# The stores of a finished token block: from SyncE's DMA queue to GpSimd's

## The chip, the cores and the metric

The kernel runs on one core of a Trainium2 chip. The metric is the time of one execution on the device, in microseconds, from the first to the last instruction of the core. Engines: PE is TensorE's matmul, PEld its weight load, DVE is VectorE, ACT is ScalarE, POOL is GpSimd, SP is SyncE. SyncE computes nothing here; it issues transfers.

## The reference, cut to what matters

```
x: (2048, 512); C_re, C_im: (2048, 2048); D_re, D_im: (512, 512); w1, w3: (512, 1376); w2: (1376, 512)
a = C_re @ (x @ D_re.T) - C_im @ (x @ D_im.T)          # real part of a two-dimensional Fourier transform
b = (silu(x @ w1) * (x @ w3)) @ w2                      # gated feed-forward half
g = sigmoid((x * gate_w).sum(-1))                       # one gate for each token
out = g * a + (1 - g) * b                               # (2048, 512), float32
```

The kernel swaps the order of the two transforms: it forms Z = C x first (the sequence transform, re and im), and then y = Z D.

## The kernel before, in words

A float32 product is made of three TensorE passes. Each operand v is split into hi (v rounded to fewer bits, a ScalarE copy, L77) and lo = v - hi (a VectorE subtraction, L83), and hi*hi + hi*lo + lo*hi is accumulated in PSUM (`mm3`, L87). So whatever TensorE reads has passed through ScalarE and VectorE first.

The program has three stages. The first is the feed-forward half, which ends at about 339 us of the span and leaves b in a DRAM buffer, `bsp`. The second is the sequence transform, from 339 to 652 us. The third is y = Z D with the gated sum.

The sequence transform works on four blocks of 512 tokens (tb). A block has 16 steps: g = 0 with p = 0 to 7 and g = 1 with p = 0 to 7. Each step multiplies one group of rows of the sequence matrix, in Winograd's form of Strassen's algorithm, so that a block makes seven products P1 to P7; g = 0 feeds P1, P3, P6, P5 (24 TensorE passes in a step) and g = 1 feeds P2, P7, P4 (18 passes). `fourier_step(n)` for step n does four kinds of work in the program's text:

- `load_c(n + 4)` loads 768 KB of the matrix: `cu` (512 KB, L445 or L448) and `cv` (256 KB, L446 or L449), both on SyncE's queue. They go into staging tiles of one pool of 13 buffers (`f4`), which other loads share.
- `sums_c(n + 2)` forms sums of the loaded parts on VectorE (L469, L470 for g = 0; L472, L473 for g = 1).
- `prep_c1(n + 2)` and `prep_c2(n + 2)` split the results into the tiles `zo` (four buffers) which TensorE reads.
- `zprod` issues TensorE's products.

At the last step of g = 0, ScalarE copies P1 into `s1` (shown as zs, L542), and VectorE forms `u2` (zu, L556), `u4` (zu, L558) and `c12` (c, L561); c12 is finished and stored by `spill` (L520). At the last step of g = 1, VectorE adds P7, P2 and P4 (L583, L584, L587, L590), and u4, s1 and u2 are stored in that order. Each of the four stores writes a tile of 128 x 1024 float32, 512 KB, to the DRAM buffer `zsp`. The tiles s1, u2, u4 and c12 have one buffer each (pool `ut`), so the next block may write such a tile only after its store has read it. The output tiles `o` of the last stage use the same four buffers.

`zsp` is read back by `load_z` (L609, tile zr) for the third stage: the first rows during the last steps of the fourth block, the others while y is computed. There `bsp` is loaded into `o` (L650), scaled by ScalarE (L651), and VectorE forms the output (L653), which goes out on ScalarE's queue and, for the last half tile, SyncE's.

The order of the instructions on each engine is set when the program is built: a scheduler places them by priority and by when buffers come free, and each engine then runs its list in that order. A DMA issue waits at the head of its engine's queue until its data and its buffer are ready, and everything behind it on that engine waits too. Each DMA also uses one of eight semaphores in turn, so it waits until the DMA eight places before it has landed. GpSimd issues no DMA before the change.

Of the kernel before, what the change touches and what calls it, by code (L numbers as in the profile page):

```python
# [12 lines left out]
P = 128  # L13
S = 2048
D = 512
# [13 lines left out]
def fnet_swiglu_gate_kernel(  # L29
# [9 lines left out]
    gw: bass.AP,  # L39
    out: bass.AP,  # L40
):
    """A float32 product is three passes: each operand v is split exactly into
    hi = v rounded to 12 significant bits and lo = v - hi, and hi*hi + hi*lo +
    lo*hi is accumulated in float32.

    The gate and up products are one 2x2x2 block product (gate | up weights by
    halves of D by two token blocks) in the seven products of Winograd's form of
    Strassen's algorithm, and so is the transform along the sequence (halves of
    D by halves of the sequence by re | im)."""
    nc = tc.nc  # L50

    def pool(name, bufs, side, space=None):
        kw = {} if space is None else {"space": space}
        cm = tc.tile_pool(name=name, bufs=bufs, side=side, reuse_waits="tile", **kw)
        return cm, cm.__enter__()
# [14 lines left out]
    def bank(k, name):  # L70
        return psum.tile([P, 512], F32, tag=f"ps{k}", name=name)

    def wide(name):
        return f4.tile([P, 1024], F32, tag="f4", name=name)

    def split(hi, lo, src, neg=False):
        nc.scalar.activation(hi, src, AF.Copy, scale=-1.0 if neg else 1.0)  # L77
        if neg:
            nc.vector.scalar_tensor_tensor(
                lo, src, -1.0, hi.bitcast(F32), op0=ALU.mult, op1=ALU.subtract  # L80
            )
        else:
            nc.vector.tensor_sub(lo, src, hi.bitcast(F32))  # L83

    def mm3(ps, ah, al, bh, bl, first, last, chain=False):
        for n, (u, v) in enumerate(((ah, bh), (ah, bl), (al, bh))):
            nc.tensor.matmul(ps, u, v, start=first and n == 0, stop=last and n == 2,  # L87
                             skip_group_check=chain)
# [5 lines left out]
    bsp = dram.tile([S, D], F32, tag="bsp", name="bsp")  # L94
    zsp = dram.tile([4 * NTB * P, 1024], F32, tag="zsp", name="zsp")

# [1 line left out]
    XO, ST = {}, {}  # L98

    def load_xo(g, t, j):  # L100
        """Half j of the staged operands t of token blocks 2g and 2g+1."""
        if g not in ST:
            ST[g] = [[wide(f"xs{g}_{q}_{i}") for i in range(4)] for q in range(2)]
            XO[g] = [xo.tile([P, 2, 7, 512], F32R, tag="xo", name=f"xo{g}_{q}") for q in range(2)]
        for q in range(2):
            nc.sync.dma_start(ST[g][q][t][:, j * 512 : (j + 1) * 512],
                              xt[g, q, :, t * 1024 + j * 512 : t * 1024 + (j + 1) * 512])

    # moving operands B11 B21 B22 T1 T2 T3 -T4 and where they are staged
    AT = {"B12": (0, 0), "B11": (0, 1), "B21": (1, 0), "B22": (1, 1),  # L110
          "T1": (2, 0), "T2": (2, 1), "T3": (3, 0), "T4": (3, 1)}
    OPS = ("B11", "B21", "B22", "T1", "T2", "T3", "T4")
# [25 lines left out]
                          w13[i % NC, :, lo * 256 : hi * 256])  # L138

    def prep_wa(i, lo=0, hi=3):  # L140
        """A11 A12 A22"""
        if lo == 0:
            WA[i] = wo.tile([P, 2, 3, 256], F32R, tag="wa", name=f"wa{i}", bufs=LOOK + 1)
        t = WA[i]
        split(t[:, 0, lo:hi].rearrange("p a n -> p (a n)"),
              t[:, 1, lo:hi].rearrange("p a n -> p (a n)"),
              WS[i][:, lo:hi].rearrange("p a n -> p (a n)"))

    def prep_wb(i, part=None):
        """S1 S2 S3 S4"""  # L150
        if part != 1:
            w = WS.pop(i)
            u = wo.tile([P, 4, 256], F32, tag="wu", name=f"wu{i}", bufs=1)
            nc.vector.tensor_add(u[:, 0], w[:, 3], w[:, 2])
            nc.vector.tensor_sub(u[:, 1], u[:, 0], w[:, 0])
            nc.vector.tensor_sub(u[:, 2], w[:, 0], w[:, 3])
            nc.vector.tensor_sub(u[:, 3], w[:, 1], u[:, 1])
            WB[i] = u
        if part != 0:
            u = WB[i]  # L160
            t = wo.tile([P, 2, 4, 256], F32R, tag="wb", name=f"wb{i}")
            split(t[:, 0].rearrange("p a n -> p (a n)"), t[:, 1].rearrange("p a n -> p (a n)"),
                  u.rearrange("p a n -> p (a n)"))
            WB[i] = t

    def prod(ps, i, wi, xi, start, chain=False):
        g = i // NC
        w, wi = (WA[i], wi) if wi < 3 else (WB[i], wi - 3)
        for q in range(2):
            sl = slice(q * P, (q + 1) * P)  # L170
            x = XO[g][q]
            mm3(ps, w[:, 0, wi, sl], w[:, 1, wi, sl], x[:, 0, xi, :], x[:, 1, xi, :],
                start and q == 0, q == 1, chain)
# [8 lines left out]
        G[i] = (x, s1)  # L182

    def first2(i):
        """the gate of the first block is P1 + P2"""
        y = bank(4 + i % 2, f"Y{i}")
        prod(y, i, 1, 1, True)
        s1 = G[i][1]
        nc.vector.tensor_add(s1, s1, y)
        nc.scalar.activation(s1, s1, AF.Silu)  # L190
# [88 lines left out]
    nc.scalar.activation(score[:, :1], warm[:, :1], AF.Silu)  # L279

    def plain(b12, a21):
        """The first chunk in eight products: they need no sums."""
        c = {}

        def half(i, j, w, x, start):
            if start:
                c[i, j] = bank((0, 4, 6, 7)[2 * i + j], f"C{i}{j}")
            for r in range(2):
                sl = slice(r * P, (r + 1) * P)
                mm3(c[i, j], w(0, sl), w(1, sl), x(r, 0), x(r, 1), start and r == 0,  # L290
                    not start and r == 1)

        def wa(k):
            return lambda h, sl: WA[0][:, h, k, sl]

        def xb(k):
            return lambda q, h: XO[0][q][:, h, k, :]

        w21 = lambda h, sl: a21[:, h, sl]
        x12 = lambda q, h: b12[:, h, q * 512 : (q + 1) * 512]  # L300
        s1 = tp.tile([P, 512], F32, tag="s1", name="s1_0", bufs=LOOK + 2)
        g1 = tp.tile([P, 512], F32, tag="g1", name="g1_0")
        h = wide("h0")
        H[0] = h
        yield half(0, 0, wa(0), xb(0), True)
        yield half(1, 0, w21, xb(0), True)
        half(0, 0, wa(1), xb(1), False)
        nc.scalar.activation(s1, c[0, 0], AF.Silu)
        yield half(1, 0, wa(2), xb(1), False)
        nc.vector.tensor_mul(h[:, :512], s1, c[1, 0])  # L310
        half(0, 1, wa(0), x12, True)
        yield half(1, 1, w21, x12, True)
        half(0, 1, wa(1), xb(2), False)
        nc.scalar.activation(g1, c[0, 1], AF.Silu)
        half(1, 1, wa(2), xb(2), False)
        yield nc.vector.tensor_mul(h[:, 512:], g1, c[1, 1])

    load_w(0, 0, 1)
    load_xo(0, 0, 1)
    load_w(0, 1, 4)  # L320
    load_xo(0, 1, 0)
    load_xo(0, 0, 0)
    load_w(1)
    load_xo(0, 1, 1)
# [4 lines left out]
    b12 = dn.tile([P, 2, 1024], F32R, tag="ho", name="b12")  # L329
    a21 = dn.tile([P, 2, 512], F32R, tag="w2o", name="a21")  # L330
    step = plain(b12, a21)
    prep_wa(0, 0, 1)
    split_xo(0, "B11")
# [72 lines left out]
    gate_up(NC, 2 * NC)  # L406
    close(xo_cm, wo_cm, tp_cm)

# [1 line left out]
    # rows d (halves) by [re | im] columns t, reduced over s (halves)  # L410
    a2_cm, a2 = pool("a2", 1, "left")
    zo_cm, zo = pool("zo", 4, "left")
    a1_cm, a1 = pool("a1", 1, "left")
# [3 lines left out]
    def flat(ap):  # L417
        return ap.rearrange("p a n -> p (a n)")

    def load_a(p):  # L420
        """A11 S1 S2 S4 | A12 A22 S3 of the rows s of tiles p and p + 8."""
        r = wide(f"xr{p}").rearrange("p (a n) -> p a n", a=4)
        m = wide(f"xm{p}").rearrange("p (a n) -> p a n", a=4)
        nc.sync.dma_start(flat(r), xn[p])
        a21, a11, a12, a22 = (r[:, i] for i in range(4))
        nc.vector.tensor_add(m[:, 0], a21, a22)
        nc.vector.tensor_sub(m[:, 1], m[:, 0], a11)
        nc.vector.tensor_sub(m[:, 2], a12, m[:, 1])
        nc.vector.tensor_sub(m[:, 3], a11, a21)
        split(A1[p][:, 0, 0], A1[p][:, 1, 0], a11)  # L430
        split(flat(A1[p][:, 0, 1:4]), flat(A1[p][:, 1, 1:4]), flat(m[:, 0:3]))
        split(flat(A2[p][:, 0, 0:2]), flat(A2[p][:, 1, 0:2]), flat(r[:, 2:4]))
        split(A2[p][:, 0, 2], A2[p][:, 1, 2], m[:, 3])

    steps = [(tb, g, p) for tb in range(NTB) for g in range(2) for p in range(NG)]
    RAW, T2, ZO = {}, {}, {}
# [80 lines left out]
    load_c(3)  # L517

    def spill(tb, k, t):
        nc.sync.dma_start(zsp[(tb * 4 + k) * P : (tb * 4 + k + 1) * P, :], t)  # L520

    U = {"banks": {k: order[2 * n : 2 * n + 2] for n, k in enumerate(("P1", "P3", "P6", "P5"))}}

# [68 lines left out]
                prep_c1(n + 2)  # L592
                prep_c2(n + 2)

# [1 line left out]
    DW, ZY = [], {}  # L596

    def load_d(q):
# [21 lines left out]
    for n in range(N1, len(steps)):  # L620
        fourier_step(n)
        k = n - N1
# [94 lines left out]
```

## Time and profile before

| | before |
|---|---|
| three runs | 742.9, 743.92, 747.85 us (median 743.92) |
| span of the profiled execution | 742.8 us |
| the profiled execution's own time beside its span | no other time is recorded for it; the span is its time, and is 0.1 us under the fastest of the three runs |
| TensorE busy | 731.3 us |
| VectorE busy | 541.0 us |
| ScalarE busy | 336.5 us |
| GpSimd busy | 0.2 us |
| DMA from SyncE's queue | 107.89 MB |

A busy time sums the instructions of an engine. A row of the timeline has the start, the length, the engine, the line, the operation with its output and inputs, the count, and in brackets the idle time of the engine before it with what ended that time. TensorE's products are pipelined: each is drawn longer than the distance to the next. Names are the program's, without buffer numbers: zu stands for u2 and u4, zs for s1, c for c12.

### The profile page before, as it was taken

The numbers are of one execution on the slowest core, as the hardware profiler recorded it, in microseconds if no ns is written. First come the engines' busy times: TensorE is split into PE (matmuls) and PEld (weight loads), VectorE is DVE, ScalarE is ACT, GpSimd is POOL, SyncE is SP. The second block draws the span as 40 slices with busy tenths as digits, with TensorE's granted clock in tenths as the row PEclk, the third lists the DMA queues.
The fourth block names the chain that finished last, engine by engine and source line by source line (L and its number), as shares of the span: only waits on it lengthen the run. The fifth ranks groups of instructions, "written<-read, shape, count | busy, mean of one in ns | idle before, by whom it ended". The sixth has DMA issues, their size and how long they took to land.

```text
span 742.8 us, 8637 instructions
## 1 busy us (share of the span) xinstructions
PE 731.3 (98%) x3196; PEld 597.6 (80%) x3196; DVE 541.0 (73%) x793; ACT 336.5 (45%) x455; POOL 0.2 (0%) x4
## 2 busy tenths in 40 slices
PE   8999999999999999999999899999999999999998
PEld 5788888888888888888887688878887788888886
DVE  6997788792777668994986887779776978834331
ACT  6755463554554436753443344344343445523320
POOL 0000000000000000000000000000000000000000
PEclk9999999999999999999999999999999999999999
DMA  7112126532013003608656554655465647963331
GB/s 268 51 65 85 57 75 248 163 124 114 30 56 114 1 28 113 210 32 313 225 172 224 197 182 146 220 189 203 153 213 172 217 163 244 350 241 114 114 107 63
DMA packets 40378, 112.50 MB, mean 151 GB/s; under 512 B 4368, under 2 KB 4752, under 8 KB 40336
## 3 DMA queue, kind: packets, MB, share of 16 engines
q1 hardware_dynamic: 38032, 107.89, 42.1%
q10 hardware_dynamic: 2304, 4.06, 1.5%
q8 instruction: 25, 0.41, 0.2%
q14 instruction: 17, 0.14, 0.1%
HBM read 95.16 MB, written 16.78 MB: 151 GB/s over the span
## 4 chain that ended last, share of the span: by engine, by line
PE 82%; DVE 8%; DMA 8%; issue 1%; ACT 1%; SPq 0%; DVEq 0%; ACTq 0%
PE P L87 26%; PE acc L87 16%; PE X L87 16%; PE y L87 12%; PE Z L87 8%; DMA cv<-cc 7%; DVE zo L83 5%; PE Y L87 4%; PE C L87 1%; DVE cv L469 1%; DMA xs<-xt 1%; DVE cv L470 1%; DVE zu L583 1%; DMA cu<-cc 1%; DVE zu L584 0%
## 5 line engine op out<-in xcount | busy, mean ns | idle before, releaser
L87 PE MATMUL P<-zo,a 128*128 128x512 f32 x1344 | 307.7, 390 | 5.6 <-DVE zo L83 4.8
L87 PEld LDWEIGHTS P<-zo,a 128*128 128x128 f32 x1344 | 251.4, 188 | 61.8 <-DVE zo L83 7.6
L87 PE MATMUL acc<-w2o,ho 128*128 128x512 f32 x528 | 120.1, 389 | 0.0
L77 ACT ACTIVATE zo<-cu 128x1024 fp32r<-128x1024 f32 x64 | 67.9, 1060 | 111.9 <-PE P L87 82.8
L87 PEld LDWEIGHTS acc<-w2o,ho 128*128 128x128 f32 x528 | 99.1, 188 | 20.7
L87 PE MATMUL X<-xo,wb 128*128 128x512 f32 x378 | 93.8, 390 | 0.0
L87 PE MATMUL y<-d,zy 128*128 128x512 f32 x384 | 87.2, 389 | 0.0
L87 PEld LDWEIGHTS y<-d,zy 128*128 128x128 f32 x384 | 72.1, 188 | 15.0
L77 ACT ACTIVATE zo<-cv 128x512 fp32r<-128x512 f32 (+1 forms) x80 | 56.2, 715 | 61.7 <-PE P L87 50.8
L87 PEld LDWEIGHTS X<-xo,wb 128*128 128x128 f32 x378 | 70.6, 188 | 15.6 <-DVE u L206 0.5
L83 DVE TENSOR_TENSOR zo<-cu,zo 128x1024 fp32r<-128x1024 f32 x64 | 78.2, 1222 | 2.6 <-ACT zo L77 2.5
L83 DVE TENSOR_TENSOR zo<-cv,zo 128x512 fp32r<-128x512 f32 (+1 forms) x80 | 62.3, 796 | 4.0 <-ACT zo L77 4.0
L83 DVE TENSOR_TENSOR zy<-zr,zy 128x1024 fp32r<-128x1024 f32 x16 | 19.5, 1225 | 40.6 <-ACT zy L77 36.3
L469 DVE TENSOR_TENSOR cv<-cv,cu 128x512 f32<-128x512 f32 x32 | 21.8, 694 | 33.6 <-DMA cv<-cc 33.6
L77 ACT ACTIVATE zy<-zr 128x1024 fp32r<-128x1024 f32 x16 | 16.8, 1056 | 44.7 <-PE y L87 43.1
L77 ACT ACTIVATE wa<-ws 128x768 fp32r<-128x768 f32 (+2 forms) x23 | 18.8, 818 | 33.6 <-PE Z L87 32.0
L87 PE MATMUL X<-xo,wa 128*128 128x512 f32 x126 | 32.7, 391 | 0.0
L87 PE MATMUL Y<-xo,wa 128*128 128x512 f32 x126 | 32.5, 389 | 0.0
L87 PE MATMUL Z<-xo,wb 128*128 128x512 f32 x126 | 32.3, 389 | 0.0
L87 PE MATMUL Z<-xo,wa 128*128 128x512 f32 x126 | 32.2, 389 | 0.0
L83 DVE TENSOR_TENSOR wb<-wu,wb 128x1024 fp32r<-128x1024 f32 x21 | 25.7, 1225 | 8.2 <-ACT wb L77 8.1
L472 DVE TENSOR_TENSOR cu<-cv,cu 128x512 f32<-128x512 f32 x32 | 22.1, 691 | 12.6 <-DMA cv<-cc 11.1
(84 smaller groups left out, 661.2 us busy)
## 6 DMA issues: line engine op xcount, KB each, us to landing
cu<-cc SPq DMA_DIRECT2D x64, 512.0 KB, 4.5
cv<-cc SPq DMA_DIRECT2D x64, 256.0 KB, 3.8
ws<-w SPq DMA_DIRECT2D x21, 512.0 KB, 3.2
zr<-zsp SPq DMA_DIRECT2D x16, 512.0 KB, 6.0
w2r<-w SPq DMA_DIRECT2D x10, 512.0 KB, 4.1
xs<-xt SPq DMA_DIRECT2D x16, 256.0 KB, 5.3
sr<-xs SPq DMA_DIRECT2D x8, 512.0 KB, 4.2
bsp<-b SPq DMA_DIRECT2D x8, 512.0 KB, 3.0
```

The lines of the kernel that those rows point to most:

```text
L77: nc.scalar.activation(hi, src, AF.Copy, scale=-1.0 if neg else 1.0)
L83: nc.vector.tensor_sub(lo, src, hi.bitcast(F32))
L87: nc.tensor.matmul(ps, u, v, start=first and n == 0, stop=last and n == 2, skip_group_check=chain)
L469: nc.vector.tensor_sub(v[:, :512], v[:, :512], b11)
L470: nc.vector.tensor_sub(T2[tb, p], b22, v[:, :512])
L472: nc.vector.tensor_sub(u[:, :512], v[:, :512], u[:, :512])
L583: nc.vector.tensor_add(u4[:, r], u4[:, r], U["P7"][r])
```

## The change

`spill` issues its transfer on GpSimd instead of SyncE. The comments and docstrings that the full diff takes out change nothing in the program.

```
     def spill(tb, k, t):
-        nc.sync.dma_start(zsp[(tb * 4 + k) * P : (tb * 4 + k + 1) * P, :], t)
+        nc.gpsimd.dma_start(zsp[(tb * 4 + k) * P : (tb * 4 + k + 1) * P, :], t)
```

It is called four times in each of the four blocks, from the last steps of g = 0 and g = 1:

```
                    nc.vector.tensor_add(c12[:, r], u4[:, r], U["P3"][r])
                spill(tb, 2, flat(c12))
...
                spill(tb, 3, flat(u4))
...
                spill(tb, 0, flat(s1))
...
                spill(tb, 1, flat(u2))
```

In the built program SyncE issues 16 transfers fewer and GpSimd 16 more, in the same sequence. TensorE's order is the same. On VectorE, L472 and L473 trade places once in each of the blocks one to three, and near the end of the fourth block a few splits on VectorE and ScalarE trade places with their neighbours.

## The prediction

> **What bounds the kernel now.** I read four views: the page's busy shares and chain, TensorE's timeline over the sequence transform, the waits of SyncE's queue, and the timelines of VectorE and SyncE around the stores.
>
> ```profile
> span 742.8 us, 8637 instructions
> PE 731.3 (98%) x3196; PEld 597.6 (80%) x3196; DVE 541.0 (73%) x793; ACT 336.5 (45%) x455; POOL 0.2 (0%) x4
> ...
> PEclk9999999999999999999999999999999999999999
> ...
> PE 82%; DVE 8%; DMA 8%; issue 1%; ACT 1%; SPq 0%; DVEq 0%; ACTq 0%
> ```
>
> TensorE has work for 98% of the span at full granted clock, and 82% of the chain that ended last is its own. SyncE's queue holds 0% of that chain. So a change off TensorE pays only where TensorE stops, and these are its stops in the sequence transform:
>
> ```profile
> 339.65 59.35 PE L87 MATMUL P<-zo,a 128*128 128x512 f32 x261
> 400.21 8.50 PE L87 MATMUL P<-zo,a 128*128 128x512 f32 x36 [1.21 <-DVE zo L83]
> 409.41 4.38 PE L87 MATMUL P<-zo,a 128*128 128x512 f32 x18 [0.70 <-DVE zo L83]
> 414.95 6.19 PE L87 MATMUL P<-zo,a 128*128 128x512 f32 x26 [1.17 <-DVE zo L83]
> 421.42 70.57 PE L87 MATMUL P<-zo,a 128*128 128x512 f32 x310 [0.28 <-DVE zu L584]
> 492.38 6.23 PE L87 MATMUL P<-zo,a 128*128 128x512 f32 x26 [0.39 <-DVE zo L83]
> 498.85 66.62 PE L87 MATMUL P<-zo,a 128*128 128x512 f32 x292 [0.24 <-DVE zu L584]
> 565.87 4.37 PE L87 MATMUL P<-zo,a 128*128 128x512 f32 x18 [0.39 <-DVE zo L83]
> 571.19 6.19 PE L87 MATMUL P<-zo,a 128*128 128x512 f32 x26 [0.95 <-DVE zo L83]
> 577.66 74.41 PE L87 MATMUL P<-zo,a 128*128 128x512 f32 x327 [0.27 <-DVE zu L584]
> 651.91 87.20 PE L87 MATMUL y<-d,zy 128*128 128x512 f32 x384
> ```
>
> The columns are start, length, what, and in brackets the idle time with its releaser. Six stops wait for a split of the sequence matrix (zo): 1.21+0.70+1.17+0.39+0.39+0.95 = 4.81 us. Three wait for VectorE to empty a bank at the turn of a block (zu): 0.79 us. The last row gives the pace, 87.20/384 = 0.227 us a product, while a product is drawn 0.39 long; each stop therefore costs 0.16 more than its bracket. The zo stops are worth 4.81+6x0.16 = 5.8 us, the zu stops 1.3 us, together 7.1 us. That is all a perfect sequence transform could gain. The fourth block has no stop at all after 577.66.
>
> **The change part by part.** Sixteen stores of 512 KB leave SyncE's queue, four per block, and go out of GpSimd's.
>
> *SyncE's queue.* What the stores cost there:
>
> ```profile
> SPq L520 <- DVE zu L583: 17.5, 4, 8.1
> ...
> SPq L520 <- DVE zs L587: 5.6, 4, 1.4
> ...
> SPq L520 <- DVE zu L590: 3.2, 4, 0.8
> SPq L520 <- DVE c L561: 3.2, 4, 0.8
> ```
>
> 29.5 us of waiting at the head of the queue that brings the sequence matrix looks like the prize. It is not, because of what stands behind them. First the store of c, in the first block (VectorE and SyncE rows together, in order of time):
>
> ```profile
> 387.11 0.69 DVE L83 TENSOR_TENSOR zo<-cv,zo 128x512 fp32r<-128x512 f32 x1
> 387.22 0.33 SPq L520 DMA_DIRECT2D zsp<-c  x1
> ...
> 387.83 0.33 SPq L449 DMA_DIRECT2D cv<-cc  x1
> ...
> 390.65 0.69 DVE L473 TENSOR_TENSOR cv<-cu,cv 128x512 f32<-128x512 f32 x1
> ...
> 391.37 0.33 SPq L445 DMA_DIRECT2D cu<-cc  x1
> 392.27 0.69 DVE L472 TENSOR_TENSOR cu<-cv,cu 128x512 f32<-128x512 f32 x1 [0.93 <-DMA cv<-cc]
> 392.88 1.22 DVE L83 TENSOR_TENSOR zo<-cu,zo 128x1024 fp32r<-128x1024 f32 x1
> ...
> 396.48 0.69 DVE L469 TENSOR_TENSOR cv<-cv,cu 128x512 f32<-128x512 f32 x1 [1.78 <-DMA cv<-cc]
> ```
>
> The load cv at 387.83 needs a staging buffer that the split at 387.11 frees; that split ends at 387.11+0.69 = 387.80, after the c on which the store waits. With the store gone the load still goes at 387.83. Now the other three, at the turn of the first block:
>
> ```profile
> 420.68 0.68 DVE L584 TENSOR_TENSOR zu<-zu,P 128x512 f32<-128x512 f32 x1
> 420.80 0.33 SPq L520 DMA_DIRECT2D zsp<-zu  x1
> ...
> 423.67 1.23 DVE L83 TENSOR_TENSOR zo<-cu,zo 128x1024 fp32r<-128x1024 f32 x1
> 423.78 0.32 SPq L520 DMA_DIRECT2D zsp<-zu  x1
> ...
> 424.92 0.33 SPq L445 DMA_DIRECT2D cu<-cc  x1
> ```
>
> The load cu at 424.92 needs the buffer of the split at 423.67, which ends at 424.90: again later on VectorE's own list than all three sums. The built order keeps these waits in the other blocks, so the waits at L520 become waits at the loads. Removed: 16 issues of 0.33, 5.3 us of an engine off the chain. Term: 0. Were a load free to go at its predecessor's heels it would gain 0.6 us (387.22 to 387.83) at c and at the turn 4.1 us (420.80 to 424.92) and the wait ahead of it (17.5/4 = 4.4), but after the turn no stop follows for 70 us; so the bound is the first, in the three blocks with stops: -1.8 us.
>
> *The transfer.* Loads behind a store no longer queue behind its bytes on the same ring.
>
> ```profile
> cu<-cc SPq DMA_DIRECT2D x64, 512.0 KB, 4.5
> cv<-cc SPq DMA_DIRECT2D x64, 256.0 KB, 3.8
> ...
> zsp<-zu SPq DMA_DIRECT2D x8, 512.0 KB, 2.8
> ```
>
> 256 KB more cost 4.5-3.8 = 0.7 us, so a store is about 1.4 us of the engines. The cv at 387.83 landed at 392.27, 4.4 us later; free of the store it may land up to 1.4 sooner. But the bytes still move, through the same engines in the same microseconds, and the tile needed next (L469, 396.48) waits for loads issued after the store. I take 0, with -1.4 to +1.4 us per c store.
>
> *VectorE's order.* The one thing the scheduler changes that could reach TensorE, after the c store of blocks one to three:
>
> ```
> before:  L473 cv<-cu,cv ; L472 cu<-cv,cu ; L83 zo<-cu,zo
> after:   L472 cu<-cv,cu ; L473 cv<-cu,cv ; L83 zo<-cu,zo
> ```
>
> L473 ran at 390.65 in time that VectorE then spent waiting 0.93 us for cv. Behind L472 it starts at 392.88 and pushes the split to 393.49, 0.61 late; the cu load that waits for L473 slips from 391.37 to about 393.6. Behind it VectorE is idle 1.78 us before L469, which covers the 0.61, and the cu has until then to queue behind earlier loads. Without that cover it is 0.61 in each of three blocks, 1.8 us. I take 0.1. In the last block a few splits of the hidden matrix and of zsp trade places with zo splits; that block has no stop and ends in the 87.20 us of y products, so 0.
>
> *GpSimd's queue.* It had four instructions (0.2 us), so the 16 stores wait there for nobody. No row shows what a store costs when GpSimd issues it. For the store itself: its tile is next written a block on.
>
> ```profile
> 422.59 0.33 SPq L520 DMA_DIRECT2D zsp<-zs  x1
> ...
> 458.49 1.28 ACT L542 ACTIVATE zs<-P 128x512 f32<-128x512 f32 x2
> ```
>
> That leaves 36 us for a store that takes 2.8. The last block's stores hold back loads of bsp and zsp on SyncE whose first use is the output sum:
>
> ```profile
> L520 SPq DMA_DIRECT2D zsp<-zu x8: 319/320/327, 420.8 to 653.6; - x8
> ...
> 670.72 1.41 DVE L653 SCALAR_TENSOR_TENSOR o<-y,gate_t,o 128x512 f32<-128x512 f32 x2
> ```
>
> The last store starts at 653.6 and takes 2.8; that leaves 14 us. Store time up to five times the present one is hidden; term 0. For VectorE, should GpSimd's work hold it up, the hold lies between nothing and the whole 2.8 us of a store; a third of a microsecond, SyncE's issue, is the nearest row. As VectorE and GpSimd share no operand here, I take 0.
>
> *Sum.* 742.8 + 0 + 0 + 0.1 + 0 = 742.9 in the profiled execution. That execution's span is 0.1 under the fastest of the three runs (742.9, 743.92, 747.85), so nothing worth counting lies around it; the median is 1.1 above. Forecast: 742.9 + 1.1 = **744.0 us**.
>
> **The rivals.**
>
> *VectorE is held while GpSimd prepares a store (slower).* The place is the turn of a block. From 414.95 TensorE does 18 products of the old block's last step and 9 of the new one (26 are in the record), stops, and resumes at 421.42 for the remaining 15 of that step: the next step begins at 421.42+15x0.23 = 424.9, and its first split ends at 424.90. There is no margin. Two stores (420.80, 422.59) are issued before that split starts, so a hold of h per store delays TensorE by 2h at each of three turns, 6h. The c stores have 0.93+1.78 us of idle VectorE behind them and add nothing below h = 2.7. It decides from the first tenth. With h = 0.33 it is 2.0 us; with the middle of 0 and 2.8, h = 1.4, it is 8.4: 744.0+8.4 = 752.4 us. For it: VectorE's rows of the turn carry no bracket, so there is no idle time to give. Against: nothing in this trace shows GpSimd working beside VectorE.
>
> [...]
>
> *The stores slow the loads (slower, smaller).* On a ring of their own the stores no longer stand in line but take turns with loads ahead of them too. A c store that puts 1.4 us before loads on which a zo stop hangs costs 1.4 in three blocks: 748.2 us. For it: DMA cv is what VectorE waited for at 396.48. Against: the same bytes were ahead of those loads before.
>
> *The loads come earlier (faster).* If cv and the loads after it land 1.4 us sooner at each c store, 4.2 of the 5.8 us of zo stops go: 739.8 us. For it: 8% of the chain is DMA. Against: issue times are fixed by VectorE, as shown. All stops gone would be 736.9, 7.1 us off.
>
> That the stores do not move is excluded: the built order shows all 16 on GpSimd, in the same sequence.
>
> **How the numbers follow.** Forecast 60%; VectorE held 22%; loads slowed 12%; loads earlier 6%. A measurement of this kernel can tell about 1%, 7.4 us. Faster by more needs every stop gone, or a fortunate run: half of the last rival, 3%. Slower by more needs h above 7.4/6 = 1.2 us, 13 of the 22, and one of the 12: 14%. Within 1%: 83%. The range is 742.0 to 751.0: it takes in the spread of the runs, the slowed loads and holds up to 1.2 us, and leaves out some 14% above and 5% below. The forecast's own range is 742.3 to 747.
>
> **What would show it.** Right: the nine stops after 339 us stay at 5 to 7 us in total; cu and cv behind the former stores are issued within 0.1 us of the end of the same VectorE split; VectorE's 0.69 and 1.22 us rows keep their lengths beside GpSimd's stores; stores land well within 36 us. Wrong: rows of VectorE at 421 to 425 longer or apart with a stop at the new block's second step (VectorE held); cv landing over 5 us with longer zo stops (loads slowed); zo stops gone (loads earlier); or a wait for a store before zs, zu or c is rewritten.

## The result, and the profile after

| | before | after |
|---|---|---|
| median of the runs beside each other | 745.1 us (8 runs, 742.9 to 747.85) | 750.25 us (8 runs, 747.85 to 751.16) |
| span of the profiled execution | 742.8 us | 748.7 us |
| its own time | none recorded | 750.77 us |

The ratio is 1.0062, with a 95% interval of 1.0044 to 1.0080. The changed kernel is slower, by 3.3 to 6.0 us. That is less than the 1% that counted as a difference in the prediction, and 750.25 lies inside its range of 742 to 751, near the upper end. It is also 6 us above the forecast of 744.0.

The rows of the page that answer to those shown of before:

```profile
span 748.7 us, 8648 instructions
PE 735.0 (98%) x3196; PEld 598.9 (80%) x3196; DVE 540.6 (72%) x793; ACT 335.7 (45%) x455; POOL 8.9 (1%) x20
...
q0 software_dynamic: 2304, 8.39, 3.1%
...
PE 71%; DMA 14%; DVE 11%; issue 2%; ACT 1%; SPq 0%; DVEq 0%; ACTq 0%
...
L87 PE MATMUL P<-zo,a 128*128 128x512 f32 x1344 | 310.4, 392 | 7.7 <-DVE zo L83 6.9
```

The 8.39 MB of stores now stand in a queue of their own (q0), and GpSimd (POOL) has 16 instructions more. DMA has grown from 8% to 14% of the chain that ended last; four of these six points are cv loads (7% before, 11% now). TensorE's idle time before products of the sequence transform is 7.7 us; the same row of before says `5.6 <-DVE zo L83 4.8`. The timeline of TensorE shows where it sits (start, length, and in brackets the idle time before the row):

```profile
339.01 56.20 PE L87 MATMUL P<-zo,a 128*128 128x512 f32 x247
395.54 4.37 PE L87 MATMUL P<-zo,a 128*128 128x512 f32 x18 [0.33 <-DVE zo L83]
401.94 14.21 PE L87 MATMUL P<-zo,a 128*128 128x512 f32 x54 [2.02 <-DVE zo L83]
416.82 6.19 PE L87 MATMUL P<-zo,a 128*128 128x512 f32 x26 [0.67 <-DVE zo L83]
...
495.76 6.19 PE L87 MATMUL P<-zo,a 128*128 128x512 f32 x26 [1.10 <-DVE zo L83]
...
561.57 8.50 PE L87 MATMUL P<-zo,a 128*128 128x512 f32 x36 [0.99 <-DVE zo L83]
...
644.81 12.32 PE L87 MATMUL P<-zo,a 128*128 128x512 f32 x53 [0.45 <-DVE zo L83]
656.97 87.20 PE L87 MATMUL y<-d,zy 128*128 128x512 f32 x384
```

The stage from the first product of the transform to the first y product took 651.91 - 338.73 = 313.2 us before (the record starts at 338.73) and takes 656.97 - 339.01 = 318.0 now: 4.8 of the 5.9 us of span. Of the other 1.1 us, 0.3 lie ahead of the transform and 0.8 behind the first y product. The stop at about 400 us grew from 1.21 to 2.02 us, a small one of 0.33 has come ahead of it, and block 4 has one that it did not have. The longer idle time makes 2.1 of the 4.8 us; some 1.6 more are a stretch at half clock behind the stop of 2.02 us, which the last section shows.

The cause of the stop of 2.02 us is seen in SyncE's waits, grouped by the waiting line and what it waited for (total us, times, longest). First before, then after:

```profile
SPq L445 <- DVE zo L83: 10.9, 21, 1.9
...
SPq L445 <- DVE cv L473: 0.6, 3, 0.2
```

```profile
SPq L445 <- DVE zo L83: 29.8, 21, 7.2
...
SPq L445 <- DVE cv L473: 8.8, 3, 3.1
```

The first row of each pair has taken over most of the waiting that left L520 (18.9 us more, of 29.5): it stands at the load behind it now, as predicted. The second row has grown from 0.6 to 8.8 us. Three times, once in each of blocks 1 to 3, a cu load waits some 3 us for L473. VectorE and SyncE in block 1 of after, in order of time:

```profile
393.05 0.69 DVE L472 TENSOR_TENSOR cu<-cv,cu 128x512 f32<-128x512 f32 x1 [2.17 <-DMA cv<-cc]
393.66 0.68 DVE L473 TENSOR_TENSOR cv<-cu,cv 128x512 f32<-128x512 f32 x1
...
394.37 0.33 SPq L445 DMA_DIRECT2D cu<-cc  x1
395.51 0.33 SPq L446 DMA_DIRECT2D cv<-cc  x1
...
400.05 0.69 DVE L469 TENSOR_TENSOR cv<-cv,cu 128x512 f32<-128x512 f32 x1 [2.64 <-DMA cv<-cc]
```

Of the step's two loads L473 needs only cu, and it frees the staging tile of the load at 394.37. In the new order it stands behind L472, which waits 2.17 us for a cv load. So the cu load goes at 394.37 (391.37 before) and everything behind it on SyncE's queue goes later. Meanwhile the DMA engines run out of work. This is the view by windows for 394 to 395.5, before and then after; its last two columns are the DMA engines' busy share and GB/s:

```profile
394.00:395.50 1.50, 1.50 (x9) 1.23 (x8) 0.70 (x2) 1.07 (x2) 0.00 (x0) 1.00 0.91 345
```

```profile
394.00:395.50 1.50, 1.20 (x6) 0.66 (x4) 1.50 (x3) 1.20 (x2) 0.00 (x0) 1.00 0.37 138
```

The second L469 of this stretch, which waits for the cv load behind, starts at 400.05; before it was

```profile
398.33 0.69 DVE L469 TENSOR_TENSOR cv<-cv,cu 128x512 f32<-128x512 f32 x1 [0.43 <-DMA cv<-cc]
```

The split for TensorE follows L469 directly, and TensorE stops for it: the split ends at 401.88 (400.66 + 1.22), and TensorE goes on at 401.94.

### The profile page after: what moved, and what is told of

It reads as the page before. It is cut to its first block, busy times and chain, and to the rows that moved or that the text cites. A ratio compares the mean times of both kernels' runs of the same rounds, so it can differ in the third digit from the quotient of the medians.

```text
span 748.7 us, 8648 instructions
## 1 busy us (share of the span) xinstructions
PE 735.0 (98%) x3196; PEld 598.9 (80%) x3196; DVE 540.6 (72%) x793; ACT 335.7 (45%) x455; POOL 8.9 (1%) x20
## 3 DMA queue, kind: packets, MB, share of 16 engines
q0 software_dynamic: 2304, 8.39, 3.1%
## 4 chain that ended last, share of the span: by engine, by line
PE 71%; DMA 14%; DVE 11%; issue 2%; ACT 1%; SPq 0%; DVEq 0%; ACTq 0%
PE acc L87 16%; PE X L87 15%; PE P L87 15%; PE y L87 12%; DMA cv<-cc 11%; PE Z L87 8%; DVE zo L83 5%; PE Y L87 4%; PE C L87 1%; DVE cv L469 1%; DMA zr<-zsp 1%; DMA dr<-dd 1%; DVE c L561 1%; DMA xs<-xt 1%; DVE cu L472 1%
## 5 line engine op out<-in xcount | busy, mean ns | idle before, releaser
L83 DVE TENSOR_TENSOR zo<-cu,zo 128x1024 fp32r<-128x1024 f32 x64 | 78.0, 1218 | 3.2 <-ACT zo L77 3.1
L83 DVE TENSOR_TENSOR zo<-cv,zo 128x512 fp32r<-128x512 f32 (+1 forms) x80 | 62.1, 792 | 4.4 <-ACT zo L77 4.3
L83 DVE TENSOR_TENSOR zy<-zr,zy 128x1024 fp32r<-128x1024 f32 x16 | 19.5, 1223 | 40.0 <-ACT zy L77 40.0
L469 DVE TENSOR_TENSOR cv<-cv,cu 128x512 f32<-128x512 f32 x32 | 21.7, 687 | 35.3 <-DMA cv<-cc 35.3
L472 DVE TENSOR_TENSOR cu<-cv,cu 128x512 f32<-128x512 f32 x32 | 22.1, 690 | 17.0 <-DMA cv<-cc 16.6
L83 DVE TENSOR_TENSOR wb<-wu,wb 128x1024 fp32r<-128x1024 f32 x21 | 25.7, 1224 | 8.2 <-ACT wb L77 8.1
```

The lines of the kernel that those rows point to most:

```text
L469: nc.vector.tensor_sub(v[:, :512], v[:, :512], b11)
L472: nc.vector.tensor_sub(u[:, :512], v[:, :512], u[:, :512])
```

## The experiments

The theory formed on these rows: the changed order of VectorE (L472 ahead of L473) makes most of the loss; a smaller part is the mixing of the c store with the cv load on the DMA engines ('mixing': they move in the same microseconds, so the load lands later); the rest is the end of the program. The rivals are the prediction's: VectorE held by GpSimd, and a cost of the queue itself. To separate order from queue, some kernels fix the order of VectorE's (and ScalarE's) instructions to that of before or of after, whatever queue the stores are on (shortened):

```
+    for a, b in zip(order, order[1:]):      # the wanted order, instruction by instruction
+        tc.add_manual_dep(b, a, no_sync)    # b is placed behind a on the same engine; nothing waits
```

Ratios are to the kernel before on the same chip, five rounds each. The differences are between the medians, in us; a ratio is not the quotient of the two medians, so the columns can differ by a microsecond. The order is VectorE's. The turn stores are the three at the turn of a block (u4, s1, u2); cv15 is the cv load of step 15, which stands behind the c store of block 1.

| run | stores on GpSimd | order | ratio (95%) | difference |
|---|---|---|---|---|
| e1 | all 16 | before in blocks 1 to 3 | 1.0037 (1.0019 to 1.0055) | +2.8 |
| e2 | none | after in blocks 1 to 3 | 1.0035 (1.0020 to 1.0050) | +2.8 |
| e3 | 12, at the turns | before | 1.0013 (1.0000 to 1.0026) | +0.6 |
| e4 | 4, of c | after | 1.0064 (1.0042 to 1.0087) | +5.3 |
| e5 | none; c late | before | 0.9992 (0.9979 to 1.0005) | -1.0 |
| e6 | all 16 | before | 1.0030 (1.0016 to 1.0045) | +2.1 |
| e7 | none | after | 1.0041 (1.0023 to 1.0059) | +2.4 |
| e8 | 4, of c | before | 1.0002 (0.9986 to 1.0017) | +0.3 |
| e9 | all 16; other end | before | 1.0015 (0.9996 to 1.0033) | +0.2 |
| e10 | all 16 (after itself) | after | 1.0072 (1.0055 to 1.0090) | +4.9 |
| e11 | none; c late | L473 always first | 0.9992 (0.9979 to 1.0004) | -1.2 |
| e12 | none (before itself) | before | 0.9993 (0.9980 to 1.0006) | -1.0 |

The last row says how far a difference can be read: a copy of before came out 1.0 us below before.

**e1: all stores on GpSimd, the old order in blocks 1 to 3.** The order is fixed for VectorE alone.

> All sixteen stores stay on GpSimd; only VectorE's order in blocks 1 to 3 is put back to the one before, L473 ahead of L472 on cu15/cv15, cu31/cv31, cu47/cv47 (ScalarE's and VectorE's new order in block 4 stays). Theory 'order': L472 ahead of L473 holds the load of cu17 back (issue 391.37 before, 394.37 after), and that makes most of the 4.5 us that the TensorE stops grew by (8.1 to 12.6 in the transform): here the cu17 load is issued again within 0.3 us of L473's end, the stops of blocks 1 to 3 come back from 11.9 to about 8.5, and the profiled span is 748.7 - 3.4 = 745.3. Rival 'mixing': the c store on a queue of its own shares the DMA engines with the cv15 load (landing 4.97 us after issue in after, 4.42 before), whatever VectorE does: stops stay near 12 and the span at 748 to 749. Rival 'held VectorE': as after, 748.7. All three keep the 0.8 us longer end of the program and the 0.45 us stop of block 4.

The cu load is back in its place (3.5 to 3.8 us behind cv15's issue in the three blocks; 3.54 before, 6.1 to 6.4 in after). The profiled span is 746.1, 0.8 above the expectation of 'order', and the ratio falls from 1.0062 to 1.0037. By the ratios under half of the loss went, not most of it, though the two intervals touch.

**e2: the new order alone, stores on SyncE.** Nothing but L472 ahead of L473, three times.

> The stores stay on SyncE's queue as before; only VectorE's order in blocks 1 to 3 is that of after, L472 ahead of L473 at three places. Theory 'order': the cu17 load slips behind L472, which waits for cv15's load (392.25): issue at about 393 in place of 391.37, a wait at the following L469 in place of its cover, and the stops grow by about 1 us in each of three blocks: span 742.8 + 3 = 745.8 (744.8 to 747). What the prediction put on record, 0.1: 742.9. Rival 'mixing': nothing, 742.8. Rival 'held VectorE': nothing, 742.8. The end of the program stays at 0.9 us behind the last output store.

The expected 745.8 came out as 745.5, and the ratio is 1.0035. No store has moved, and half of the loss is there. SyncE's waits show the same row as after:

```profile
SPq L445 <- DVE cv L473: 8.4, 3, 3.1
```

**e3 and e4: the turn stores alone, the c stores alone.**

```
-        nc.gpsimd.dma_start(zsp[...], t)
+        (nc.sync if k == 2 else nc.gpsimd).dma_start(zsp[...], t)    # e3; e4 has the two exchanged
```

> The c store of each block goes back to SyncE, the three turn stores of each block stay on GpSimd; VectorE's order is that of before. Theory 'order' and rival 'mixing' (both place the cost at the c store): stops of blocks 1 to 3 as before (8.1), the closing list still with all eight extra semaphores: 742.8 + 0.8 = 743.6. Rival 'held VectorE': it keeps its price at the turns, six holds of about 1 us, 748 to 749. If the turn stores slow the loads of the next block instead, 745 to 747 and longer stops in the steps behind 421, 501 and 581.

> Only the c store of each block goes to GpSimd, the three turn stores stay on SyncE; VectorE's order is that of after. Theory 'order' and rival 'mixing': the same longer stops as in after (12 us in place of 8.1), and a closing list with four extra semaphores in place of eight, so 748.7 less 0.2 to 0.5: 748.3. Rival 'held VectorE' at the turns: 743 to 744, since no turn store is on GpSimd any more.

In neither was an order fixed. The turn stores alone leave VectorE's built order as it was, and the c stores alone bring the whole of the new one: it is the c store whose move swaps L472 and L473. e3 is 0 to 1.9 us slower than before, the longer end of the program included. So 'held VectorE' is out at the prediction's smallest price (0.33 us for each store, 2.0 us in all) and above. e4 is as slow as after with a quarter of its stores. It was expected 0.4 below after and is not; its profile, of the slowest of its six runs, has two stops in block 4 (0.89 and 0.77 us) that the profiles of e7 and e8, which have its parts apart, do not have. The cause of that excess is open.

**e6, e7, e8: queue and order apart.** e6 has the queue of after and the whole order of before, e7 the reverse, e8 only the c stores on GpSimd with the order of before.

> All sixteen stores on GpSimd as in after, and the whole order of VectorE and ScalarE in the transform as before: what is left is the queue alone. Sum of the theories so far, from median spans (before 744.0, all stores on GpSimd with blocks 1 to 3 in the old order 746.55): the longer end 0.86 stays, block 4's stop of 0.5 goes, the mixing of the c store with the cv15 load stays: 746.0 (745.4 to 746.4). Rival 'only the order costs': 744.0 + 0.86 = 744.9. Rival 'held VectorE': 748 or more.

> All stores on SyncE as before, and the whole order of VectorE and ScalarE in the transform as in after: what is left is the order alone. With the swap of L472 and L473 alone the median span was 746.8; if block 4's order costs 0.5 by itself: 747.3. If block 4's order costs only together with stores on GpSimd: 746.8. If order and queue add up, this and the run with the queue alone give together what after gives: (746.0 - 744.0) + (747.3 - 744.0) = 5.3 over before, against 4.2 to 5.9 measured for after; a sum well under that says that each makes the other worse.

> Only the four c stores go to GpSimd, the turn stores stay on SyncE, and the order of VectorE and ScalarE is that of before. Theory 'mixing': the c store on a queue of its own shares the engines with the cv15 load, which lands 0.5 us later after its issue, and this costs 0.3 to 0.5 in each of three blocks; with 0.15 at the end: 744.0 + 1.4 = 745.4 (744.8 to 746). Rival 'the queue costs nothing': 744.15. Rival 'the loads come earlier, since cv15 no longer waits behind the c store': 743.0 or less.

Order alone costs 0.41% (1.7 to 4.4 us), the queue alone 0.30% (1.2 to 3.4 us). Together that is 0.71%; the changed kernel itself measured 0.62% and, in e10, 0.72%. Within the intervals the two add up. Both came out under their expectations: the median spans are 745.3 in e6 (746.0 expected, 744.9 by its rival 'only the order costs') and 745.8 in e7 (747.3 or 746.8 expected). Taken by stores, e3 and e8 make only 0.15% of the queue's 0.30%; the intervals are too wide to say whether anything is missing. e8 was a miss for the theory: with the order of before, a c store on GpSimd costs 0.02%, not the 1.4 us of 'mixing'. The bytes do mix: the cv15 load landed 5.1 us after its issue in e8 and 4.4 before, and VectorE waited 1.57 us for it in place of 0.93. But with the cu load in its place TensorE's stop at 400 us did not grow (1.02 us; 1.21 before). SyncE's wait for L473 in e7 and in e6:

```profile
SPq L445 <- DVE cv L473: 8.0, 3, 3.2
```

```profile
SPq L445 <- DVE cv L473: 0.6, 3, 0.2
```

and TensorE's idle time before the transform's products, in e7 and in e8:

```profile
L87 PE MATMUL P<-zo,a 128*128 128x512 f32 x1344 | 308.2, 390 | 7.0 <-DVE zo L83 6.0
```

```profile
L87 PE MATMUL P<-zo,a 128*128 128x512 f32 x1344 | 308.1, 390 | 4.9 <-DVE zo L83 4.0
```

One such number is no measurement: e12, a second profile of before, has 4.9 there where the first has 5.6, and e6 has 7.0 with the old order. Nor is one stop: e3 has 2.05 us at 400 with the old order and the cu load in its place. The ratios carry the verdict.

**e9: the end of the program.** Of the queue's cost, part lies behind the last product. The issue of the last output store, in before, after and e9 (whose text has one line more):

```profile
740.10 0.34 SPq L655 DMA_DIRECT2D out<-o  x1
```

```profile
745.17 0.34 SPq L655 DMA_DIRECT2D out<-o  x1
```

```profile
740.39 0.34 SPq L656 DMA_DIRECT2D out<-o  x1
```

From there to the end of the span it is 742.8 - 740.1 = 2.7 us before, 748.7 - 745.2 = 3.5 in after, and 743.0 - 740.4 = 2.6 in e9 (in e6, 3.4). The store takes 1.7 us to land in each. What follows is SyncE's closing list, which waits for every semaphore that a DMA used; before and after:

```profile
L713 SPq EVENT_SEMAPHORE  x7: 17/28/1254, 740.5 to 742.7; - x7
```

```profile
L713 SPq EVENT_SEMAPHORE  x11: 17/28/28, 745.5 to 748.6; - x11
```

GpSimd's stores use eight semaphores of their own, so the list has nine waits in place of five (two of each row's count are others), and the one for the last output store stands second of nine in place of third of five. In e9 seven loads of L650 are cut in two, which moves that store to the last semaphore of the list:

```
-            nc.sync.dma_start(b, bsp[n * P : (n + 1) * P, :])
+            for h in ((slice(0, D // 2), slice(D // 2, D)) if n < 7 else (slice(0, D),)):
+                nc.sync.dma_start(b[:, h], bsp[n * P : (n + 1) * P, h])
```

> As the run with the queue alone (all stores on GpSimd, order of before), but seven of the sixteen loads of L650 are made in two halves, so that the last store of the output counts on another semaphore: the last of SyncE's closing list of waits in place of the second of nine. Theory 'place in the list': between the landing of the last output store and the end of the span lay 0.92 us before (third of five), 1.77 and 1.79 with all stores on GpSimd (second of nine), 1.05 and 1.07 where it was sixth of nine; here it is 0.8 to 0.95, and the span 0.8 to 1.0 shorter than with the queue alone, 744.4 where that had 745.25. Rival 'the longer list costs by its length': 1.7 to 1.8 as in after. What lies outside the span stays at 2.08.

The end is as short as before, and the ratio falls from 1.0030 (e6) to 1.0015, 1.1 us; the intervals overlap, but the rows above show 0.8 of it directly. The list of e9 is as long as that of e6, so the place in the list decides, not its length. With that gone, the queue alone can no longer be told from before, nor from e6. The twelve runs of e9 lie in two groups, seven at 744.5 to 746.2 us and five at 748.2 to 749.4, for which no reason was found; so the difference of medians, 0.2, says less than the ratio.

**e10 and e12: the two kernels themselves again.**

> The changed kernel itself, on the same chip as the kernels beside it. If order and queue add up, it stands 2.4 to 3.0 (order alone) and 2.1 (queue alone) over before: 4.5 to 5.1 us. If each makes the other worse, 5.5 or more.

> The kernel before, as a second profile of it and as a measure of how far two measurements of one kernel lie apart. The profiled execution of before on which the prediction rests had a span of 742.8 us, under the median spans of later runs (743.4 to 744.0), so its 8.1 us of stops in the transform should be on the low side: here 8 to 10 us, a span of 743 to 745.5, and a ratio of 1.000 within 0.002. If the stops come out at 12 or more, the growth in the changed kernel is spread and not an effect; the measured ratios stand in any case.

The changed kernel is 4.9 us over before in e10, as expected if order and queue add up. The ratio of e12 is within its 0.002, but its span, 742.4, and its idle time in the transform lie under what was expected, so nothing shows that the profile on which the prediction rests has too few stops.

**e5 and e11: a version meant to beat both.** The stores stay on SyncE, and the c store of blocks 1 to 3 moves back in SyncE's order; e11 also puts L473 ahead of L472 wherever they were neighbours.

```
-  cu15, store of c, cv15, cu16, ... cv25, cu26      # SyncE's order in block 1; 31 to 41 and 47 to 57 alike
+  cu15, cv15, cu16, ... cv25, store of c, cu26
```

> All stores on SyncE's queue, orders of VectorE and ScalarE as before; only the c store of blocks 1 to 3 is issued later, behind the second load of step 9 of the next block (near 436 in place of 387 for block 1), where the DMA engines are 30 to 50% busy and not 85 to 94%. Theory 'full DMA stretch': the stops of blocks 1 to 3 (8.1 us in the profile of before) come from loads that share 388 to 396 with 512 KB of c store at some 300 GB/s, 1.7 us of transfer; the first stop of each block shrinks by 1 to 1.4 us: median span 744.0 - 3 = 741 and the time 1.5 to 4 us lower. Rival 'buffers': the loads wait for VectorE's splits to free a buffer, a lighter DMA stretch only moves the landing of cv15, and the span stays at 743.5 to 744.5.

> All stores on SyncE, the c store of blocks 1 to 3 late as in the run before, and at the eight steps where VectorE still had L472 ahead of L473 right behind it the two change places, so that L473, which waits for cu's load alone, never stands behind a wait for cv's. Theory 'order': the load that L473's end releases is issued 0.6 us earlier or more at eight steps; each of these loads lies in a stretch where ScalarE and VectorE are ahead, and only those near a stop bring anything: span 0.3 to 1.0 under the late c store alone (742.45), 741.5 to 742.1. Rival 'only the three places at a full DMA stretch count': 742.4. Rival 'L472 late holds ScalarE's split of cu': 743 or more.

Neither can be told from before: 0.9992 in both, and 0.9993 for its copy. In the profile of e5 TensorE's idle time in the transform is 3.5 us, which is what the theory wanted, but runs of one kernel spread over more than the 2 us that this is worth. Both expectations were too hopeful. The profile of e11 has the 742.4 us that its rival named (only the three places at a full stretch count), but so has e12, the copy of before, so this decides nothing.

## Why the prediction came out as it did, step by step

**SyncE's queue, term 0: right.** At the turn of block 1 in after, VectorE's split and SyncE's load:

```profile
425.54 1.22 DVE L83 TENSOR_TENSOR zo<-cu,zo 128x1024 fp32r<-128x1024 f32 x1
...
426.78 0.33 SPq L445 DMA_DIRECT2D cu<-cc  x1
```

The load goes 0.02 us behind the split's end, as before; the waits moved from L520 to L445.

**The transfer, term 0 with 1.4 either way for each c store: right.** e8 puts it at 0.3 us between the medians, with an interval of -1.0 to +1.3, for all four c stores. So 'the stores slow the loads' (4.2 us) and 'the loads come earlier' (a gain of 4.2) are both out. By the prediction's own signs the first was nearly met: the stops grew, and the cv loads behind the c store landed after up to 5.0 us in after (5.6 in e10). The landings are the stores' doing (up to 5.2 us in e8, which has the order of before), but e8 shows that they cost nothing that can be measured.

**VectorE's order, 0.1: wrong, and this is the step that failed.** It measured 1.7 to 4.4 us (e7). The prediction saw the edit, the late cu load (about 393.6; it was 394.37) and the idle time of 1.78 us before L469, and called that idle time cover. It was not. VectorE was idle there because it waited for a DMA, and the DMA queue was the thing being delayed: the late load holds all loads behind it on SyncE, and in the 1.5 us in which it goes out the DMA engines' share is 0.37 in place of 0.91 (0.67 in e7, with the order alone). Its bound without cover, 1.8, lies within what was measured, but it priced the 0.61 us that the split slipped, and not the 3 us that the load slipped; the stop of 2.02 us ends on a cv load that stood behind the late one. Block 4's part, put at 0, is not resolved: e7 has it and e2 has not, and they differ by 0.06%.

**GpSimd, term 0: right for VectorE, short at the end of the program.** VectorE's rows beside a GpSimd store, at the turn of block 1 of after, and GpSimd's store:

```profile
422.55 0.68 DVE L584 TENSOR_TENSOR zu<-zu,P 128x512 f32<-128x512 f32 x1
```

```profile
422.94 0.53 POOL L520 DMA_DIRECT2D zsp<-zu  x1 [34.62 <-DVE zu L583]
```

The sum takes 0.68 us, as it did before, and the first split of the new block starts 2.99 us behind it, as it did before (425.54 - 422.55; 423.67 - 420.68), although two stores are issued in between; in blocks 2 and 3 it is 2.98 or 2.99 in both. 'VectorE is held' is out by these rows, by VectorE's busy time (541.0 and 540.6), and by e3. The slack for the stores held too: they land in

```profile
DMA to landing us min/median/max: 2.9/3.5/5.4
```

against 36 and 14 us of room. What the term left out is the program's end: the second queue brought eight semaphores of its own, and more of the closing list now stands behind the wait for the last store, 0.8 us in the profile of after. Outside the span 0.3 us more came with the stores (last section). What else the queue costs of its 1.2 to 3.4 us is open.

**The sum and its base: wrong by 1.2 us beside the effect.** The prediction said that nothing worth counting lies around the span, and the text ahead of it that the metric ends with the core's last instruction. In the later runs the time is 1.8 to 2.1 us above the span, so the 742.8 of the profile belongs to an execution of about 744.6, and the 743.92 taken as the median is low: later medians of before are 745.1 to 745.8. The forecast of 744.0 missed by that and by the 5 us of effect.

So the changed kernel came out within 1%, as the likeliest case said, but not for its reason. It said that nothing moves; two things moved, and together they cost less than 1%. That the time stayed inside the range, by 0.75 us, is luck: the range was made for the spread of the runs and for held or slowed engines, and neither cost is among these.

## What to carry to other kernels

When an edit changes the built order, follow the swap to the first DMA issue behind it, price how late that issue goes and what stands behind it on its queue. An engine's idle time is cover only if what ends it does not depend on the thing made late. Here another DMA queue also changed how the program ended, by 0.8 us in the profile of after, so look at the last microseconds before calling a queue free.

## What the runs showed of the hardware

In after a GpSimd store is issued in 0.53 us (SyncE: 0.33) and lands 2.9 to 5.4 us later; the latest of the other profiles took 6.8 (e8, block 4). The c store of blocks 1 to 3, beside loads, landed after 4.8 to 5.9 us from GpSimd's queue (seven profiles) and, at the same place, after 4.0 to 4.5 from SyncE's (five). In before, with loads and stores on one queue, SyncE's 257 transfers landed in the order of their issue. In after the packets of the c store and of the loads moved in the same microseconds: 122 of q0 (0.46 MB) and 116 of q1 (0.27 MB) from 390 to 392 us. The cv15 load beside it landed 4.97 us after its issue there, 4.42 in before.

After some stops of TensorE its granted clock fell to half for 3.4 us, eight products 0.43 us apart in place of 0.23, a loss of some 1.6 us on top of the stop. The windows of after, and of e2 with a longer stop; the column ahead of the last two is the clock:

```profile
399.00:402.00 3.00, 0.97 (x6) 0.47 (x4) 1.95 (x3) 1.05 (x2) 0.00 (x0) 1.00 0.33 131
...
403.00:406.50 3.50, 3.50 (x10) 2.74 (x9) 1.95 (x4) 0.41 (x1) 0.00 (x0) 0.52 0.68 203
```

```profile
399.00:402.00 3.00, 0.93 (x5) 0.43 (x3) 1.50 (x2) 1.07 (x2) 0.00 (x0) 1.00 0.48 184
...
403.00:406.50 3.50, 3.50 (x17) 2.87 (x16) 2.48 (x4) 1.06 (x1) 0.00 (x0) 1.00 0.71 243
```

The stop was 2.02 us in after and 2.46 in e2, and only the first was followed by the slow stretch; e3 (2.05; its clock was 0.54 from 403 to 406.5), e4 (1.99) and e10 (2.57) had it too: in e4 and e10 the 80 products behind the stop took 20.0 us, which is 18.4 at 0.23 each. No single stop under 1.9 us did (e7 had one of 1.87), but in e4 a second such stretch followed stops of 0.89 and 0.77 us with one product between them (53 products in 13.91 us, 12.32 in after). What decides whether a slow stretch follows, these runs do not show. Runs of before seem to have such stretches too. One takes 1.7 us (half of 3.4), or 0.002, off a run's mean granted clock, and that was 0.998 or less in 26 of the 87 runs beside e1 to e11, and these were 1.3 to 1.7 us longer than the others, by the means on each of the three chips. So a part of the spread between runs goes with it.

What lies outside the span, a run's time less its span, has a median of 1.8 us in the kernels with four GpSimd stores or none, 2.1 in those with twelve or sixteen (after, e1, e3, e6, e10), and 1.9 in e9. Why is open.
